# Row sums of softmax from added-up chunks: four chunks of E summed on Pool and split into two fp16 halves, in place of sixteen matmuls

## The chip, the cores and the metric

The kernel runs on one core of one Trainium2 chip. The metric is the device time of one execution in microseconds (us), median over several runs.

## The reference, cut to what matters

Attention with 8 batches and 12 heads, sequence 448, head size 64, then a gated feed-forward block on 3584 tokens with width 768 and inner width 1536. Inputs and output are fp32.

```python
def _attn_ref(q, k, v):
    scores = (1.0 / np.sqrt(q.shape[-1])) * np.matmul(q, k.transpose(0, 1, 3, 2))
    scores = scores - np.max(scores, axis=-1, keepdims=True)
    attn = np.exp(scores)
    attn = attn / (np.sum(attn, axis=-1, keepdims=True) + 1e-09)
    return np.matmul(attn, v)

def _moe_ref(x, w_gate, w_val, w_out):
    g = x @ w_gate
    silu = g * (1.0 / (1.0 + np.exp(-g)))
    return silu * (x @ w_val) @ w_out
```

## The kernel before

The 96 heads are taken in 48 pairs, one pair per turn of a loop of 50 turns. In a turn PE (the matmul engine, which takes its work in the program's order) makes the scores of the pair in two halves (QK), ScalarE (ACT) turns them into `E = exp(scores)` in fp16, and PE fills the time in between with steps of the feed-forward block of earlier batches (`ffn_run`). Two pairs make a "quad" of four heads. In even turns PE takes the row sums of a quad by multiplying `E` with ones, in odd turns it multiplies `E` with `v` (PV), and VectorE (DVE) scales the product with the reciprocal of the sums.

`E` has the key index on partitions, in four chunks of 112. So a row sum goes over partitions and over chunks: 4 chunks x 4 heads = 16 matmuls.

```python
    def sums(p0):
        acc = ps_f.tile([128, 512], FP32, tag="f")
        for c in range(NC):                      # 4 chunks
            for j in range(4):                   # 4 heads
                nc.tensor.matmul(acc[ts(j, 32), 0:S], lhsT=ones[:],
                    rhs=E[p0 + j // 2][:, c, j % 2, :],
                    start=(c == 0), stop=(c == NC - 1))
        R[p0] = attp.tile([128, S], FP32, tag="R", bufs=2, name="R")
        return acc

    def recips(p0, acc):
        ssb = attp.tile([128, S], FP32, tag="ssb", bufs=1)
        nc.vector.tensor_copy(ssb[:], acc[:, 0:S])
        rt = R[p0]
        return [lambda i=i: nc.vector.reciprocal(rt[:, ts(i, P)], ssb[:, ts(i, P)])
                for i in range(4)]
    # ... (cut)
        for pr in range(END):
            # ...
            if pr < NPAIR:
                qk_half(pr, 0, ...)
            if pr + 3 < NPAIR and pr + 3 >= NPE:
                prep(pr + 3)                     # Pool copies q and k of a later pair
            if not odd and 14 <= pr + LA < NPAIR:
                load_qk16(pr + LA)               # issued by Pool
            if pr + 2 < NPAIR:
                # ...
                if (pr + 2) % GP == GP - 1 and 4 <= (pr + 2) // GP + 1 < NGRP:
                    load_v((pr + 2) // GP + 1)   # issued by Pool, three buffers
            # ...
            elif not odd and pr >= 2:
                deferred.extend(recips(pr - 2, sums(pr - 2)))
            # ...
            work = odd and pr > FIRST + 1
            if work:
                pop_deferred(4)
                scaled(pr - 3, 0, pv(pr - 3, 0))
            # ...
            carry = ffn_run(state["left"] / slots + carry)
            # ...
                qk_half(pr, 1, ...)
            if work:
                scaled(pr - 3, 1, pv(pr - 3, 1))
            carry = ffn_run(state["left"] / max(1, slots - 1) + carry)
```

The softmax here doesn't subtract the row's maximum and nothing guards it: scores larger than these inputs give would overflow.

## Time and profile before

| before | value |
|---|---|
| time, median of 4 runs | 462.67 us (462.06 to 463.93) |
| span of the profiled run | 460.2 us |
| busy PE / VectorE / ACT / Pool | 452.3 / 236.8 / 243.0 / 104.2 us |
| PE idle (span less busy) | 7.9 us, nearly all in the first 30 us |

A line of the waits view names the engine and instruction that waited, what released it, and then total us, number of times and longest wait. This is all that PE waits for in the kernel before:

```profile
PE s L196 <- ACT E L203: 2.2, 5, 0.4
PE wp L103 <- DVE ones L355: 1.2, 1, 1.2
PE acc L234 <- ACT E L203: 0.4, 1, 0.4
PE s L196 <- DVE qkT L175: 0.2, 1, 0.2
```

The windows view gives the busy time of each engine in a stretch of time (instructions in brackets), then PEclk, the share of full speed that PE's clock was granted. For before, in two stretches of the later part:

```profile
85.00:113.00 28.00, 28.00 (x390) 11.82 (x382) 19.32 (x29) 16.64 (x22) 9.49 (x16) 1.00 1.08 140
113.00:167.00 54.00, 54.00 (x950) 28.05 (x952) 32.39 (x51) 30.94 (x44) 15.45 (x25) 1.00 0.70 93
```

PE (second number) is busy for every microsecond, at full clock; VectorE (fourth) is busy for 60 to 70%; Pool (sixth) for about 30%.

### The profile page before, as it was taken

Reading aid. Unit: us, or ns where it says so; the run is one execution under the profiler, and the core shown is the slowest. Engines: PE = TensorE matmul, PEld = TensorE weight load, DVE = VectorE, ACT = ScalarE, POOL = GpSimd, SP = SyncE. Lnnn points to the kernel's source line nnn. Section 1 sums busy time; section 2 is a strip of 40 time slices with the busy share of each in tenths; the row PEclk is TensorE's granted clock in tenths of the full one; section 3 lists DMA queues with packets and bytes.
Section 4 is the critical chain, followed back from the end, with each engine's and each line's share of the span. In section 5 each row is a group of like instructions: output and inputs, shape, how many; then the busy total and the mean of one; then the engine's idle time right before and its main releaser. Section 6 shows DMA issues by size and latency. Waiting matters only on the chain.

```text
span 460.2 us, 14133 instructions
## 1 busy us (share of the span) xinstructions
PE 452.3 (98%) x6367; PEld 227.8 (49%) x6367; DVE 236.8 (51%) x371; ACT 243.0 (53%) x353; POOL 104.2 (23%) x164
## 2 busy tenths in 40 slices
PE   8899999999999999999999999999999999999996
PEld 3344444444455555444455555544445556554454
DVE  2765663666764554564654554636555546334310
ACT  7986666656664555454646555455555562222222
POOL 8455606334150132303123040210200000000000
PEclk9999999999999999999999999999999999999999
DMA  9999999995793484662758393903603111100123
GB/s 133 195 200 201 192 180 183 223 154 80 90 113 57 78 126 49 114 102 31 118 58 119 67 131 74 142 6 76 98 10 56 37 37 36 36 11 25 36 68 103
DMA packets 82045, 44.23 MB, mean 96 GB/s; under 512 B 36673, under 2 KB 78529, under 8 KB 81985
## 3 DMA queue, kind: packets, MB, share of 16 engines
q0 software_dynamic: 42368, 23.37, 39.2%
q1 hardware_dynamic: 39520, 19.92, 23.8%
q8 instruction: 49, 0.80, 0.7%
q14 instruction: 12, 0.09, 0.1%
q10 hardware_dynamic: 96, 0.05, 0.0%
HBM read 47.19 MB, written 11.01 MB: 126 GB/s over the span
## 4 chain that ended last, share of the span: by engine, by line
PE 95%; ACT 3%; DMA 1%; DVE 0%; issue 0%; SPq 0%; ACTq 0%
PE gp L264 15%; PE op L261 14%; PE vp L264 13%; PE vp L261 11%; PE op L264 10%; PE s L196 10%; PE gp L261 9%; PE acc L212 9%; PE acc L234 4%; ACT E L203 2%; DMA rk<-in_k_dram 1%; PE tp L184 1%; PE wp L103 0%; PE tp L167 0%; DVE qkT L175 0%
## 5 line engine op out<-in xcount | busy, mean ns | idle before, releaser
L203 ACT ACTIVATE E<-s 112x896 f16<-112x896 f32 x192 | 164.6, 917 | 24.3 <-PE s L196 24.1
L280 ACT ACTIVATE sg<-gp 128x384 f32<-128x384 f32 (+1 forms) x96 | 52.3, 545 | 85.4 <-PE gp L264 54.7
L292 DVE SCALAR_TENSOR_TENSOR t<-sg,gp 128x384 f32<-128x384 f32 (+1 forms) x96 | 58.5, 610 | 64.3 <-ACT sg L280 64.2
L325 ACT ACTIVATE osb<-op 128x384 f32<-128x384 f32 (+1 forms) x57 | 27.7, 486 | 100.5 <-PE op L261 56.3
L264 PE MATMUL gp<-X,wg 128*32 128x512 f16 (+1 forms) x1416 | 78.1, 355 | 0.0
L249 DVE RECIPROCAL R<-ssb 128x112 f32<-128x112 f32 x92 | 73.1, 827 | 0.7
L295 DVE SCALAR_TENSOR_TENSOR hts<-t,vp 128x384 f16<-128x384 f32 (+1 forms) x96 | 59.6, 621 | 23.3 <-PE vp L264 7.9
L261 PE MATMUL op<-wo,hts 128*128 128x384 f16 (+1 forms) x408 | 68.6, 322 | 0.0
L264 PE MATMUL vp<-X,wv 128*32 128x512 f16 (+1 forms) x1224 | 66.9, 353 | 0.0
L226 DVE TENSOR_TENSOR X<-acc,R 128x448 f16<-128x448 f32 x48 | 29.7, 624 | 64.9 <-PE acc L212 63.1
L261 PE MATMUL vp<-X,wv 128*128 128x384 f16 (+1 forms) x270 | 58.4, 352 | 0.0
L196 PE MATMUL s<-qkT 64*128 64x448 f16 x384 | 54.8, 355 | 2.5 <-ACT E L203 2.2
L261 PEld LDWEIGHTS <-hts 128*128 128x128 f16 x408 | 38.9, 98 | 28.2 <-issue 3.0
L264 PEld LDWEIGHTS <-wg 128*32 128x32 f16 x1416 | 37.8, 97 | 29.6
L264 PE MATMUL op<-wo,hts 128*32 128x384 f16 x1104 | 48.9, 326 | 0.0
L261 PE MATMUL gp<-X,wg 128*128 128x384 f16 (+1 forms) x222 | 47.4, 350 | 0.0
L264 PEld LDWEIGHTS <-wv 128*32 128x32 f16 x1224 | 32.7, 97 | 25.5
L212 PE MATMUL acc<-E,vt 112*32 112x448 f16 x768 | 45.2, 355 | 0.0
L126 POOL DMA_DIRECT2D vt<-in_v_dram x16 | 12.3, 772 | 142.7 <-PE acc L212 141.7
L261 PEld LDWEIGHTS <-wv 128*128 128x128 f16 x270 | 25.3, 98 | 26.9 <-issue 4.8
L264 PEld LDWEIGHTS <-hts 128*32 128x32 f16 x1104 | 29.5, 97 | 16.3
L154 POOL COPY qk<-q 112x512 f16<-112x512 f16 x37 | 22.9, 620 | 63.9 <-DMA qkT<-qk 46.4
(38 smaller groups left out, 201.2 us busy)
## 6 DMA issues: line engine op xcount, KB each, us to landing
vt<-in_v_dram POOLq DMA_DIRECT2D x16, 336.0 KB, 5.2
q<-in_q_dram POOLq DMA_DIRECT2D x22, 224.0 KB, 5.9
k<-in_k_dram POOLq DMA_DIRECT2D x22, 224.0 KB, 6.7
out_dram<-osb SPq DMA_DIRECT2D x7, 336.0 KB, 3.1
wg<-in_moe_w_gate_dram POOLq DMA_DIRECT2D x8, 288.0 KB, 11.1
wv<-in_moe_w_val_dram POOLq DMA_DIRECT2D x8, 288.0 KB, 11.4
wo<-in_moe_w_out_dram POOLq DMA_DIRECT2D x2, 1152.0 KB, 21.6
out_dram<-osb SPq DMA_DIRECT2D x8, 288.0 KB, 2.9
```

The costliest lines, as they stand in the source:

```text
L154: nc.gpsimd.tensor_copy(dst, src)
L196: nc.tensor.matmul(s[:, hx, 0:S], lhsT=t[ts(hx, 64)].rearrange("p c q -> p (c q)")[:, c * P : c * P + 128], rhs=t[ts(hx, 64), NC:, :].rear ...
L203: nc.scalar.activation(E[pr][:, c], s[0:P, :, 0:S], AF.Exp, scale=sm_scale)
L212: nc.tensor.matmul(acc[ts(j, 32), 0:S], lhsT=v16[g][:, 2 * r + j % 2, c, :].rearrange("p (d t) -> p t d", t=2)[:, t], rhs=E[p0 + j // 2][: ...
L226: nc.vector.tensor_tensor(X[kk][:, hp + t, ts(bb, S)], acc[:, 0:S], R[p0][:], ALU.mult)
L249: lambda i=i: nc.vector.reciprocal(rt[:, ts(i, P)], ssb[:, ts(i, P)]) for i in range(4)
L261: nc.tensor.matmul(dst, lhsT=lhsT, rhs=rhs, start=start, stop=stop)
L264: nc.tensor.matmul(dst[ts(j, 32), :], lhsT=lhsT[:, ts(j, 32)], rhs=rhs, start=start, stop=stop)
L280: nc.scalar.activation(sg[:, 0:n], gp[:, 0:n], AF.Tanh, scale=0.5)
L292: nc.vector.scalar_tensor_tensor(t1[:, 0:n], sg[:, 0:n], 1.0, gp[:, 0:n], ALU.add, ALU.mult)
L295: nc.vector.scalar_tensor_tensor(hts[:, fb, 0:n], t1[:, 0:n], 0.5 * HS, vp[:, 0:n], ALU.mult, ALU.mult)
L325: nc.scalar.activation(osb[:, ds(m0, w)], op[:, 0:w], AF.Copy, scale=1.0 / HS)
```

## The change

The intent is to take row-sum work off PE, the bound. For pairs 12 to 47 the four chunks of a head are first added elementwise on Pool in fp32. The sum is then written as two fp16 halves, because the row-sum matmuls here read fp16: ACT rounds a quarter of it (`hi`), VectorE makes the remainder (`lo`), and PE multiplies both with 4.0. That takes 8 matmuls rather than 16. To give this chain time, sums and PV of the later quads come one turn later (odd and even change places). To give Pool time, the copies of q and k go to VectorE. Space in SBUF is found by smaller buffers (RB 5 to 4, no `t1`), and k of pair 0 is loaded on ACT's queue.

```diff
-RB = 5
+RB = 4
+PS = 12
@@ copies of q and k in prep
-                    nc.gpsimd.tensor_copy(dst, src)
+                    (nc.vector if pr >= PS + 3 else nc.gpsimd).tensor_copy(dst, src)
@@
+    def presum_a(pr):
+        ts_ = [attp.tile([P, S], FP32, tag="tsum", bufs=3, name="tsum") for _ in range(2)]
+        tsum[pr] = ts_
+        for hx in range(2):
+            nc.gpsimd.tensor_tensor(ts_[hx][:], E[pr][:, 0, hx], E[pr][:, 1, hx], ALU.add)
+
+    def presum_b(pr):
+        for hx in range(2):
+            t = tsum[pr][hx]
+            for c in (2, 3):
+                nc.gpsimd.tensor_tensor(t[:], t[:], E[pr][:, c, hx], ALU.add)
+
+    def presum_hi(pr):
+        hl[pr] = attp.tile([P, 2, 2, S], FP16, tag="hl", bufs=2, name="hl")
+        for hx in range(2):
+            nc.scalar.activation(hl[pr][:, 0, hx], tsum[pr][hx][:], AF.Copy, scale=0.25)
+
+    def presum_lo(pr, hx):
+        nc.vector.scalar_tensor_tensor(
+            hl[pr][:, 1, hx], tsum[pr][hx][:], 0.25, hl[pr][:, 0, hx], ALU.mult, ALU.subtract
+        )
@@ in sums(): n chunks rather than NC
+        pre = p0 >= PS
+        n = 2 if pre else NC
+                src = hl[p0 + j // 2] if pre else E[p0 + j // 2]
@@ the loop
+            elif odd and pr >= PS + 3 and pr - 3 < NPAIR:
+                pop_deferred(99)
+                deferred.extend(recips(pr - 3, sums(pr - 3)))
+            if PS < pr <= NPAIR:
+                presum_b(pr - 1)
-            work = odd and pr > FIRST + 1
+            quad = None
+            if odd and FIRST + 1 < pr < PS + 3:
+                quad = pr - 3
+            if not odd and pr >= PS + 4:
+                quad = pr - 4
+            work = quad is not None
@@ after the second half of PV
+            if PS <= pr < NPAIR:
+                presum_a(pr)
+            if PS < pr <= NPAIR:
+                presum_hi(pr - 1)
+                for hx in range(2):
+                    deferred.append(lambda p=pr - 1, hx=hx: presum_lo(p, hx))
@@ (cut: END = NPAIR + 3, add_at one turn later, t1 replaced by sg, ones with a 4.0, loads of pair 0 and of q16/k16 rearranged)
```

More of the change, by code (lines that the diff above doesn't have):

```diff
@@ L64, in load_table @@
         )
-    load_table("natural_log_exp_and_others")
     consts = ctx.enter_context(tc.tile_pool(name="consts", bufs=1))
@@ L77 @@
     ps_f = ctx.enter_context(tc.tile_pool(name="ps_f", bufs=3, space=PSUM))
-    ones = consts.tile([P, 32], FP16, name="ones")
-    warm = consts.tile([128, 512], FP16, name="warm")
+    ones = consts.tile([P, 2, 32], FP16, name="ones")
+    warm = ep.tile([128, 512], FP16, tag="E", name="warm")
     ident = consts.tile([P, P], FP16, name="ident")
@@ L93 @@
     raw = {}
+    pairbuf = []
+    tsum = {}
+    hl = {}
     v16 = {}
@@ L107, in load_qk32 @@
         rk = raws.tile([P, 2, NC, D], FP32, tag="rk", bufs=RB)
-        for dst, src in ((rq, q), (rk, k)):
-            nc.sync.dma_start(dst[:], src[0, 2 * pr : 2 * pr + 2].rearrange("h (p c) d -> p h (c d)", c=NC))
+        for dst, src, eng in ((rq, q, nc.sync), (rk, k, nc.scalar)):
+            eng.dma_start(dst[:], src[0, 2 * pr : 2 * pr + 2].rearrange("h (p c) d -> p h (c d)", c=NC))
         raw[pr] = (rq[:], rk[:])
     def load_qk16(pr, n=2):
-        q16 = raws.tile([P, 4, NC, D], FP16, tag="rq", bufs=RB, name="q16")
-        k16 = raws.tile([P, 4, NC, D], FP16, tag="rk", bufs=RB, name="k16")
-        for dst, src in ((q16, q), (k16, k)):
+        h0 = 2 if pr == 2 else 0
+        if h0 == 0:
+            pairbuf.clear()
+            for tag in ("rq", "rk"):
+                pairbuf.append(raws.tile([P, 4, NC, D], FP16, tag=tag, bufs=RB, name=tag))
+        for dst, src in zip(pairbuf, (q, k)):
             flat = src.rearrange("b h s d -> (b h) s d")[2 * pr : 2 * pr + 2 * n]
-            nc.gpsimd.dma_start(dst[:, 0 : 2 * n], flat.rearrange("h (p c) d -> p h (c d)", c=NC))
+            nc.gpsimd.dma_start(
+                dst[:, h0 : h0 + 2 * n], flat.rearrange("h (p c) d -> p h (c d)", c=NC)
+            )
         for i in range(n):
-            raw[pr + i] = (q16[:, 2 * i : 2 * i + 2], k16[:, 2 * i : 2 * i + 2])
+            raw[pr + i] = tuple(x[:, h0 + 2 * i : h0 + 2 * i + 2] for x in pairbuf)
     def load_v(g, lo=0, hi=2 * GP):
@@ L228, in scaled @@
         )
+    def presum_a(pr):
[15 more added lines that the diff above has]
+            hl[pr][:, 1, hx], tsum[pr][hx][:], 0.25, hl[pr][:, 0, hx], ALU.mult, ALU.subtract
+        )
     def sums(p0):
         acc = ps_f.tile([128, 512], FP32, tag="f")
-        for c in range(NC):
+        pre = p0 >= PS
+        n = 2 if pre else NC
+        for c in range(n):
             for j in range(4):
+                src = hl[p0 + j // 2] if pre else E[p0 + j // 2]
                 nc.tensor.matmul(
                     acc[ts(j, 32), 0:S],
-                    lhsT=ones[:],
-                    rhs=E[p0 + j // 2][:, c, j % 2, :],
+                    lhsT=ones[:, int(pre)],
+                    rhs=src[:, c, j % 2, :],
                     start=(c == 0),
-                    stop=(c == NC - 1),
+                    stop=(c == n - 1),
                 )
@@ L290, in ffn1_steps @@
                 )
-            t1 = fp.tile([128, 512], FP32, tag="t1")
             nc.vector.scalar_tensor_tensor(
-                t1[:, 0:n], sg[:, 0:n], 1.0, gp[:, 0:n], ALU.add, ALU.mult
+                sg[:, 0:n], sg[:, 0:n], 1.0, gp[:, 0:n], ALU.add, ALU.mult
             )
             nc.vector.scalar_tensor_tensor(
-                hts[:, fb, 0:n], t1[:, 0:n], 0.5 * HS, vp[:, 0:n], ALU.mult, ALU.mult
+                hts[:, fb, 0:n], sg[:, 0:n], 0.5 * HS, vp[:, 0:n], ALU.mult, ALU.mult
             )
@@ L353 @@
         load_qk32(0)
+        load_table("natural_log_exp_and_others")
         nc.vector.memset(warm[:], 0.0)
-        nc.vector.memset(ones[:], 1.0)
+        nc.vector.memset(ones[:, 0], 1.0)
+        nc.vector.memset(ones[:, 1], 4.0)
         load_qk16(1, 1)
@@ L428 @@
         carry = 0.0
-        DELAY = 2
-        END = NPAIR + 2
+        END = NPAIR + 3
         add_at = {FIRST: 0}
         for i in range(1, B - 1):
-            add_at[NHP * (i + 1) + DELAY] = i
+            add_at[NHP * (i + 1) + (2 if NHP * i + 4 < PS else 3)] = i
         for pr in range(END):
@@ L461 @@
                 ffn_run(2.5)
-            elif not odd and pr >= 2:
+            elif not odd and 2 <= pr < PS + 2:
                 deferred.extend(recips(pr - 2, sums(pr - 2)))
@@ L470 @@
                     scaled(pr - 3, t, halves[t])
-            work = odd and pr > FIRST + 1
+            if PS < pr <= NPAIR:
[6 more added lines that the diff above has]
+            work = quad is not None
             if work:
-                pop_deferred(4)
-                scaled(pr - 3, 0, pv(pr - 3, 0))
+                pop_deferred(99)
+                scaled(quad, 0, pv(quad, 0))
             if pr in add_at and pr != FIRST:
@@ L495 @@
             if work:
-                scaled(pr - 3, 1, pv(pr - 3, 1))
+                scaled(quad, 1, pv(quad, 1))
+            if PS <= pr < NPAIR:
[4 more added lines that the diff above has]
+                    deferred.append(lambda p=pr - 1, hx=hx: presum_lo(p, hx))
             tiled[0] = pr >= TILED and work
```

## The prediction

> **What bounds the kernel now.** I read first the table of busy time and the page's chain that ended last, then the waits of PE and of Pool, then the timelines of PE and Pool in the middle of the run.
>
> ```profile
> PE 452.3 (98%) x6367; PEld 227.8 (49%) x6367; DVE 236.8 (51%) x371; ACT 243.0 (53%) x353; POOL 104.2 (23%) x164
> PE 95%; ACT 3%; DMA 1%; DVE 0%; issue 0%; SPq 0%; ACTq 0%
> ```
>
> The chain is PE for 95% of the span. Since a busy PE need not be an efficient one, I checked with the waits of PE: they add up to 4.0 us (exponentials 2.6, a memset 1.2, a copy 0.2), and in the window from 30 us to the end there is none at all. After the first 28 us, in which the exponentials pace the chain, every microsecond taken from PE shortens the run and every microsecond for which PE is made to wait lengthens it: there is no slack to absorb either.
>
> The row sums in PE's timeline (start us, length us; four chunks times four heads are the 16 matmuls):
>
> ```profile
> 158.05 0.55 PE L196 MATMUL s<-qkT 64*128 64x448 f16 x4
> 158.53 0.94 PE L212 MATMUL acc<-E,vt 112*32 112x448 f16 x16
> 159.30 2.13 PE L264 MATMUL op<-wo,hts 128*32 128x384 f16 x48
> 161.25 1.15 PE L264 MATMUL vp<-X,wv 128*32 128x384 f16 x24
> 162.33 0.55 PE L196 MATMUL s<-qkT 64*128 64x448 f16 x4
> 162.81 0.94 PE L234 MATMUL acc<-E,ones 112*32 112x448 f16 x16
> ```
>
> Lengths overlap, so I take start to start: a set of sums (L234) 162.81 to 163.58, where the next group starts, 0.77 us; PV is also 0.77, a gate or value step of 384 columns 0.98 (1.30 of 512), an output step 1.95, a QK half 0.5. A pair (one turn of the loop) takes some 9 us.
>
> Pool in the same stretch (the bracket is the idle time before):
>
> ```profile
> 159.77 0.77 POOL L126 DMA_DIRECT2D vt<-in_v_dram  x1 [27.42 <-PE acc L212]
> 160.53 0.62 POOL L154 COPY qk<-q 112x512 f16<-112x512 f16 x1
> 161.08 0.62 POOL L154 COPY qk<-k 112x512 f16<-112x512 f16 x1
> ```
>
> This is the row that decides my prediction. Pool stood for 27 us at the issue of a V load until the last PV that reads the old V buffer was over (159.30 on PE; 0.47 us later the issue starts), and the copies behind it had to stand too. Pool's waits give 141.7 us in 9 such places. Today this costs nothing, since Pool is 23% busy and what stands behind is needed much later.
>
> **What the Trainium skill says.** (1) "GPSIMD Engine Reference", section 3.1: a two-input tensor_tensor costs about 2.6 cycles per element at 1.2 GHz (4497 ns for 2048 fp32), a one-input body 1.03. The trace agrees with the second: copies of 512 start 555 ns apart, 439 ns of which is 512 x 1.03 / 1.2, leaving 116 ns for the instruction. The first the trace before can't test, as it has no two-input Pool instruction. Estimate for 448 elements: 448 x 2.55 / 1.2 + 116 = 1070 ns. (2) "SBUF — State Buffer", section "Who interferes with whom": a VectorE instruction with two SBUF inputs, or in a 2-port mode, and a GpSimd instruction that reads SBUF block each other for a whole instruction. Before, no costly VectorE group has two SBUF inputs, so the trace doesn't show it. (3) "TensorE: Matmul & The Clock Gate", Part 1: after an idle window of about 3.4 us the clock falls to half. The trace has PEclk at 9 throughout and no PE wait over 1.2 us, so it is silent too.
>
> **The change part by part.** Eighteen quads (pairs 12 to 47) get their sums from 8 matmuls instead of 16: 384 become 240. Saved on PE: 18 x 0.77 / 2 = **6.9 us**, all on the path. At the start, k goes out on ACT's queue beside q: the cast of k waited until 4.30 us against 3.59 for q, and VectorE is busy with q until 3.98, so some **0.3 us**. Wider gaps elsewhere: none; the feed-forward work is only shifted by one pair.
>
> Added off PE: Pool 216 adds x 1.07 = 231 us, less 66 copies x 0.62 = 41 that go to VectorE, so Pool rises to about 294 us. Per 9 us pair that is 6 x 1.07 + about 1.0 of DMA issue = 7.4 us: full, but below the bound. ACT 72 copies x 0.58 (the nearest row is 128x448 at 577 ns) = 42 us, to 285. VectorE 72 subtractions x 0.6 = 43 plus 66 copies x about 0.3 = 20, to 300. By sums of busy time nothing passes PE, and one would expect about 455.
>
> The order of instructions says otherwise. A pair's last four adds (its two remaining chunks, two heads) stand on Pool **behind the V load** of their turn. In turns 18, 24, 30, 36 and 42 that load waits for the second PV half of the very same turn, because PV of the new quads now comes one turn later (in turn p+4 instead of p+3) while the V load and its three buffers stayed. And these four adds are needed by the row sums early in the next turn. So a chain appears, from the end of that PV: release 0.47 + V issue 0.77 + four adds 4.28 + ACT's rounding to fp16 0.6 + VectorE's remainder 0.6 with some 0.5 of blocking by Pool = 7.2 us, then the sums on PE. Meanwhile PE has in its fixed order, by the program:
>
> - turn 18: value and gate steps of 512 columns, QK: 1.30 + 1.30 + 0.5 = 3.1, wait 4.1
> - turns 30 and 42: value of 512, output, QK: 1.30 + 1.95 + 0.5 = 3.8, wait 3.4 each
> - turns 24 and 36: output, value (2.9), then a gate step whose PSUM buffer is freed by an ACT copy that stands behind the two rounding copies: 0.47 + 0.77 + 4.28 + 0.6 + 0.5 = 6.6, wait 3.7 each
>
> Sum: 4.1 + 2 x 3.4 + 2 x 3.7 = **18.3 us** of new PE idle time.
>
> A second, weaker loop: three sum buffers for two heads a pair make the second first-add of a pair wait for the previous pair's remainder, which on VectorE stands behind reciprocals; in even turns the issue of q and k (1.4 us) comes between. Turn by turn this mostly fits into the 9 us; in the shortest, turn 20 (6.6 us of PE work), I count a wait of up to 3.8 us. I put **2 us** in for all of this, a choice: the other turns could add to it, and VectorE may be earlier than I think.
>
> Sum: 462.5 - 6.9 - 0.3 + 18.3 + 2 = 475.6; I say **475 us**.
>
> **The rivals.**
> (a) *All hidden.* The adds are much faster than my estimate. At 0.5 us each the chain of the V load is 4.9 us, its waits shrink to about 1.8, 1.1, 1.1 and twice 1.4, in all 7 us, and the run takes some 462; at 0.3 us it is nearly hidden, 457 or so. For it: sums of busy time leave room everywhere, and the change looks as if its author thought of latency (sums and PV come later, casts leave Pool). Against it: the copy's 555 ns for one input, and the page's rate for two.
> (b) *The shared port.* Per pair VectorE has two subtractions with two SBUF inputs and two copies that may need the port while Pool is at it for 6.4 us; every one can lose up to 1.07 us, so VectorE 300 + 36 x 4 x 0.5 = 372 us. Then remainders and feed-forward products come late as well, PSUM buffers come free late, and the time is 480 to 490. For it: the page. Against: VectorE's total still lies under PE's.
> (c) *The clock falls* after those idle times of over 3.4 us: 5 times up to 1.7 us more, near 484. For it: their length; against: they are just at the page's window.
> (d) *Pool becomes the bound*: it needs the adds at 1.35 us or more (6 x 1.35 + 1.0 = 9.1 per pair). Then over 480.
>
> **Range and chances.** The step that carries all is the length of an add: a tenth of a microsecond of it is worth 4 x 5 x 0.1 = 2 us. With 0.3 to 0.5 us we are at 456 to 462, with 0.9 to 1.2 at 472 to 480, with (b) or (c) up to 490. Range 455 to 490. Faster by over 2% means below 453.3, more than the 7.2 us that there is to win: 0.05. Within 2% is rival (a), which an author who measured would have wanted to see: 0.35. Slower (above 471.8): 0.60.
>
> **What would show it.** Right: PE's waits list the sums' matmuls waiting for VectorE or ACT, about 3 to 4 us in each of five places some 54 us apart, with a V issue on Pool just before; the mean of a Pool tensor_tensor is about 1.07 us; the chain runs through Pool in those places; a set of sums takes about 0.39 us start to start. Wrong: adds of under 0.5 us, or PE without waits after 30 us; then the time is 455 to 460. If the waits of PE are spread over all turns instead of five, the second loop or the shared port was the larger term; a PEclk below 9 after the gaps would be rival (c).

## The result, and the profile after

| | before | after |
|---|---|---|
| median | 462.67 us | 516.94 us (514.85 to 519.04, 4 runs) |
| span of the profiled run | 460.2 us | 515.0 us |
| PE busy / idle | 452.3 / 7.9 us | 469.6 / 45.4 us |
| VectorE busy | 236.8 us | 334.3 us |
| ACT busy | 243.0 us | 275.1 us |
| Pool busy | 104.2 us | 302.0 us |
| mean granted clock | 1.00 | 0.966 |

The ratio is 1.1169, 95% interval 1.1118 to 1.122: slower by 11.7%. A ratio here is always the mean time of one kernel's runs over that of the other's runs of the same rounds, so it isn't quite the ratio of the medians quoted.

The prediction said slower, but 475 us and at most 490. Of the 54.8 us by which the span grew, 37.5 are PE's idle time (45.4 less 7.9) and 17.3 are more busy time. PE's busy time should have fallen by 6.9, so some 24 us of slower work are hidden in it. One part is the clock (below). The matmuls' ends are modelled, so another part may be a tail put on the last matmul ahead of each wait; that is not shown.

The chain that ended last, by engine, in the kernel after:

```profile
PE 65%; DVE 12%; POOL 10%; ACT 7%; issue 4%; DMA 1%; POOLq 0%; DVEq 0%; ACTq 0%
```

Before, PE had 95% of it. The three largest waits of PE after:

```profile
PE acc L267 <- ACT hl L253: 12.8, 8, 2.0
PE acc L267 <- DVE hl L256: 10.2, 10, 3.3
PE gp L297 <- ACT osb L357: 7.4, 2, 3.7
```

L267 is the matmul of the row sums, L253 the rounding, L256 the remainder. Their 23.0 us are waits for the new chain. The 7.4 us on `osb` are the two turns that the prediction gave 3.7 us each, at its very numbers. Added up by place from PE's timeline, the five turns with a V load wait 2.8, 3.7, 2.5, 3.7 and 2.5 = 15.2 us (predicted 18.3). But some 20 us lie in other turns, where I had counted 2.

First such a turn with a V load, turn 18. Pool (start us, length, then what; the bracket is the idle time before and what ended it):

```profile
126.72 0.77 POOL L134 DMA_DIRECT2D vt<-in_v_dram  x1 [1.03 <-PE acc L220]
127.50 4.51 POOL L248 TENSOR_TENSOR tsum<-tsum,E 112x448 f32<-112x448 f32 x4
```

And PE in the same stretch:

```profile
125.69 0.74 PE L220 MATMUL acc<-E,vt 112*32 112x448 f16 x12
126.25 1.47 PE L297 MATMUL vp<-X,wv 128*32 128x512 f16 x24
127.55 1.47 PE L297 MATMUL gp<-X,wg 128*32 128x512 f16 x24
128.95 0.55 PE L204 MATMUL s<-qkT 64*128 64x448 f16 x4
129.43 0.37 PE L267 MATMUL acc<-hl,ones 112*32 112x448 f16 x2
130.32 0.35 PE L267 MATMUL acc<-hl,ones 112*32 112x448 f16 x1 [0.52 <-ACT hl L253]
132.68 0.56 PE L267 MATMUL acc<-hl,ones 112*32 112x448 f16 x4 [2.01 <-ACT hl L253]
133.54 0.53 PE L267 MATMUL acc<-hl,ones 112*32 112x448 f16 x1 [0.30 <-DVE hl L256]
133.55 2.75 PE L297 MATMUL vp<-X,wv 128*32 128x512 f16 x23
```

PV ends, Pool issues the V load, makes four additions, and only then come rounding, remainder and sums. PE has value, gate and QK in between, as predicted, and waits. The last row shows a second loss: the value step (23 of its 24 matmuls lie in the stretch) takes 2.75 us where the same step took 1.47 seven rows above.

Now a turn without a V load, turn 17, on PE:

```profile
110.99 0.37 PE L267 MATMUL acc<-hl,ones 112*32 112x448 f16 x4 [2.01 <-ACT hl L253]
113.83 0.53 PE L267 MATMUL acc<-hl,ones 112*32 112x448 f16 x1 [2.47 <-DVE hl L256]
113.84 3.09 PE L297 MATMUL gp<-X,wg 128*32 128x512 f16 x24
116.37 2.76 PE L297 MATMUL vp<-X,wv 128*32 128x512 f16 x24
```

PE waits 2.0 us for a rounding and 2.5 us for a remainder, and the two feed-forward steps behind them start 2.5 us apart instead of 1.30. The windows view says why (first number after the comma PE's busy time, PEclk is third from the end); the stretches are cut where the granted clock changes:

```profile
108.40:111.81 3.41, 0.95 (x9) 0.29 (x8) 1.19 (x2) 1.63 (x4) 3.33 (x4) 1.00 0.18 24
111.81:118.63 6.82, 4.80 (x48) 2.61 (x48) 6.03 (x8) 1.82 (x3) 5.85 (x6) 0.50 0.37 22
118.63:122.00 3.37, 3.37 (x35) 1.12 (x30) 2.83 (x6) 2.53 (x4) 0.00 (x0) 1.00 0.14 29
```

The clock was at half from 111.81 to 118.63 us. It fell 0.4 us into the second wait, so the first wait and the little work around it were enough. The whole run has seven such falls, ahead of the drop at its end: in the five turns with a V load, in turn 17 and in turn 21. They begin at 111.81, 132.29, 152.77, 197.14, 258.58, 320.02 and 381.46 us, whole multiples of 3.41 us apart, and in the 3.41 us ahead of each PE was busy for 0.00 to 1.40 us. Two such slots in turn 15, with 1.67 and 2.00 us of work, were not followed by a fall. In all the clock was at half for 34.1 us, and PE was busy for 27.6 of them; so, as an estimate, the clock cost PE at most 27.6 / 2 = 14 us of its own time.

Over the longer stretches shown of before, after has:

```profile
85.00:113.00 28.00, 20.17 (x257) 8.10 (x250) 19.02 (x29) 17.18 (x25) 24.40 (x25) 0.98 0.73 98
113.00:167.00 54.00, 45.00 (x523) 20.27 (x526) 40.40 (x60) 26.46 (x42) 37.89 (x39) 0.82 0.41 53
```

Last, the groups of instructions (busy us in total, mean ns of one, then idle time before them and what ended it):

```profile
L256 DVE SCALAR_TENSOR_TENSOR hl<-tsum,hl 112x448 f16<-112x448 f32 x72 | 53.6, 764 | 34.7 <-ACT hl L253 34.5
L162 DVE COPY qk<-rq 112x512 f16<-112x512 f16 x33 | 31.7, 962 | 1.9 <-DMA rq<-in_q_dram 1.9
...
L162 DVE COPY qk<-rk 112x512 f16<-112x512 f16 x33 | 25.1, 761 | 0.9 <-DMA rk<-in_k_dram 0.9
```

```profile
L253 ACT ACTIVATE hl<-tsum 112x448 f16<-112x448 f32 x72 | 39.4, 583 | 37.7 <-POOL tsum L248 37.6
```

```profile
L248 POOL TENSOR_TENSOR tsum<-tsum,E 112x448 f32<-112x448 f32 x144 | 153.4, 1076 | 5.9
L242 POOL TENSOR_TENSOR tsum<-E 112x448 f32<-112x448 f16 x72 | 84.2, 1176 | 75.0 <-DVE hl L256 75.0
```

An addition onto a sum (L248) takes 1076 ns (1070 predicted), a first addition (L242) 1176; the median of all is 1041. A copy of q takes 962 ns and one of k 761 on VectorE, where I had put 0.3 us. And Pool waits 75 us for remainders, which free the sum buffers: the second loop of the prediction is there. Read as a circle: first additions wait for remainders (75.0 us), roundings for additions (37.6 us), remainders for roundings (34.5 us).

### The profile page after: what moved, and what is told of

Same layout as the page of the kernel before. It is cut to its first block, busy times and chain, and to the rows that moved or that the text cites. A ratio compares the mean times of both kernels' runs of the same rounds, so it can differ in the third digit from the quotient of the medians.

```text
span 515.0 us, 14492 instructions
## 1 busy us (share of the span) xinstructions
PE 469.6 (91%) x6331; PEld 235.5 (46%) x6331; DVE 334.3 (65%) x510; ACT 275.1 (53%) x425; POOL 302.0 (59%) x314
## 4 chain that ended last, share of the span: by engine, by line
PE 65%; DVE 12%; POOL 10%; ACT 7%; issue 4%; DMA 1%; POOLq 0%; DVEq 0%; ACTq 0%
PE op L294 11%; PE gp L297 11%; PE vp L294 8%; POOL tsum L248 8%; PE vp L297 8%; PE gp L294 6%; PE s L204 6%; PE acc L220 6%; PE op L297 5%; ACT E L211 4%; DVE hl L256 3%; DVE qk L162 3%; PE acc L267 2%; ACT hl L253 2%; DVE sg L324 2%
## 5 line engine op out<-in xcount | busy, mean ns | idle before, releaser
L248 POOL TENSOR_TENSOR tsum<-tsum,E 112x448 f32<-112x448 f32 x144 | 153.4, 1076 | 5.9
L242 POOL TENSOR_TENSOR tsum<-E 112x448 f32<-112x448 f16 x72 | 84.2, 1176 | 75.0 <-DVE hl L256 75.0
L297 PE MATMUL gp<-X,wg 128*32 128x512 f16 (+1 forms) x1440 | 89.7, 380 | 11.8 <-ACT osb L357 7.4
L324 DVE SCALAR_TENSOR_TENSOR sg<-sg,gp 128x384 f32<-128x384 f32 (+1 forms) x96 | 58.0, 604 | 49.3 <-ACT sg L313 48.9
L297 PE MATMUL vp<-X,wv 128*32 128x512 f16 (+1 forms) x1296 | 77.1, 368 | 0.3 <-DVE ssb L279 0.3
L256 DVE SCALAR_TENSOR_TENSOR hl<-tsum,hl 112x448 f16<-112x448 f32 x72 | 53.6, 764 | 34.7 <-ACT hl L253 34.5
L327 DVE SCALAR_TENSOR_TENSOR hts<-sg,vp 128x384 f16<-128x384 f32 (+1 forms) x96 | 59.6, 621 | 15.9 <-PE vp L294 3.9
L357 ACT ACTIVATE osb<-op 128x384 f32<-128x384 f32 (+1 forms) x57 | 27.6, 483 | 78.2 <-PE op L294 45.6
L253 ACT ACTIVATE hl<-tsum 112x448 f16<-112x448 f32 x72 | 39.4, 583 | 37.7 <-POOL tsum L248 37.6
L294 PE MATMUL vp<-X,wv 128*128 128x512 f16 (+1 forms) x252 | 54.7, 354 | 0.0
L297 PEld LDWEIGHTS <-wv 128*32 128x32 f16 x1296 | 39.6, 101 | 30.2 <-issue 6.7
```

What stands on the lines that cost most here:

```text
L242: nc.gpsimd.tensor_tensor(ts_[hx][:], E[pr][:, 0, hx], E[pr][:, 1, hx], ALU.add)
L248: nc.gpsimd.tensor_tensor(t[:], t[:], E[pr][:, c, hx], ALU.add)
L256: nc.vector.scalar_tensor_tensor(hl[pr][:, 1, hx], tsum[pr][hx][:], 0.25, hl[pr][:, 0, hx], ALU.mult, ALU.subtract)
L294: nc.tensor.matmul(dst, lhsT=lhsT, rhs=rhs, start=start, stop=stop)
L297: nc.tensor.matmul(dst[ts(j, 32), :], lhsT=lhsT[:, ts(j, 32)], rhs=rhs, start=start, stop=stop)
L324: nc.vector.scalar_tensor_tensor(sg[:, 0:n], sg[:, 0:n], 1.0, gp[:, 0:n], ALU.add, ALU.mult)
```

## The experiments

The theories:

- **V load**: the V load ahead of the additions makes a chain, as predicted.
- **Buffers**: three sum buffers for two heads a pair tie Pool's first additions to the remainders of the pair before, and turns grow into each other.
- **Port**: Pool's additions and VectorE's copies and remainders block each other, VectorE's in-order queue runs late, and PE waits for it in all turns.
- **Clock**: waits make PE's clock fall, so each costs more than its length.

### The rest of the change alone

```diff
-PS = 12
+PS = 48
```

No pair takes the new way; the rearranged loads, buffers and the longer loop stay.

> The sums of all pairs taken by PE from the four chunks again, all other parts of the change kept (four raw buffers, in-place feed-forward product, k loaded on ACT's queue, table load later). Theory of the chain (PE waits for sums that Pool makes late): all 54 us come from the added-up sums, so this is back at 462 to 464. Rival (the other parts cost something of their own): over 467.

Correct, 462.44 us, ratio 0.9992 (0.9965 to 1.002). The rest of the change costs and gains nothing. The 0.3 us that the prediction wanted from the earlier load of k can't be seen: in the profiles the first row of exponentials started at 6.0 and 6.8 us in the two kernels with the old way of loading, and at 6.6 to 7.3 us in the others.

### The V load at the end of its turn

```diff
-                if (pr + 2) % GP == GP - 1 and 4 <= (pr + 2) // GP + 1 < NGRP:
+                if pr < PS and (pr + 2) % GP == GP - 1 and 4 <= (pr + 2) // GP + 1 < NGRP:
                     load_v((pr + 2) // GP + 1)
@@ ahead of the last ffn_run of the turn
+            if PS <= pr < NPAIR - 2 and pr % GP == 0 and (pr + 2) // GP + 1 < NGRP:
+                load_v((pr + 2) // GP + 1)
```

> The V load of a later turn issued at the end of its turn, behind the last four adds, not before them. Chain theory: the five places where PE waits after a V load (2.8, 3.7, 2.5, 3.7, 2.5 us, 15.2 in all) go, with the clock lost behind them (about 6 us): 493 to 500. The waits of the turns 14, 16 and 20 stay. Rival (the port shared by Pool and VectorE makes everything late): still 508 or more.

Correct, 497.79 us, ratio 1.0755 (1.0722 to 1.0787). Against the changed kernel that is 0.0414 of 463 us, or 19 us. The V load was worth what the prediction gave it (18.3), its waits of 15.2 us and some clock. But 35 us remain.

### Four sum buffers

```diff
-... tag="tsum", bufs=3 ...
+... tag="tsum", bufs=4 ...
-        ssb = attp.tile([128, S], FP32, tag="ssb", bufs=1)
-        nc.vector.tensor_copy(ssb[:], acc[:, 0:S])
         rt = R[p0]
+        nc.vector.tensor_copy(rt[:], acc[:, 0:S])
@@ the reciprocals read rt in place of ssb (to find the space)
```

> Four sum buffers in place of three (room made by taking the reciprocals in place), so that the second first-add of a pair no longer waits for the previous pair's remainder. Chain theory: Pool's 75 us of waiting for VectorE go, PE's waits in the turns 15, 17 and 21 (11.6 us and 2 at a gate step) and most of the lost clock there (up to 9.7 us) go, the V waits stay: 485 to 496. Rival (shared port): VectorE's copies and remainders are as late as before, 505 or more.

Correct, 514.90 us, ratio 1.1122 (1.108 to 1.1163). The expectation of 485 to 496 failed; the gain of 2 us isn't even certain, since the intervals overlap. So the 75 us that Pool waited for remainders did not by themselves cost the time: with Pool let go, VectorE's busy time rose from 334 to 351 us, and PE waited for other things.

### Both together

> Both at once. Chain theory: PE's waits after 30 us fall from some 38 us to under 6, the clock stays near 1.00, and the saving of 6.9 us on PE comes through: 455 to 466. Rival (shared port): PE still waits over 15 us for remainders, 480 or more.

Correct, 492.82 us, ratio 1.0642 (1.0616 to 1.0667). If the two loops were the cause, the time had to come near 460. With the V load out of the way the buffer is worth 5 us (1.0755 less 1.0642), no more. VectorE's busy time is now 359.9 us, and PE waits for the whole of VectorE's work:

```profile
PE gp L296 <- DVE sg L323: 8.5, 5, 2.1
PE acc L220 <- DVE X L234: 6.3, 5, 1.7
PE acc L267 <- DVE hl L256: 6.2, 7, 1.4
```

`sg` is a feed-forward product, `X` the scaling of PV: both were there before the change and were never late. The buffer theory is out as the main cause. The port theory had asked for 480 or more, which came, and for over 15 us of waits for remainders, which did not: there were 6.2, out of 22.3 for VectorE as a whole.

### Additions that nobody reads, and the same without them

Two kernels. Their outputs are wrong, which doesn't matter for the times. In the first, Pool makes all its additions, but rounding and remainder read a constant tile, so that no work waits for an addition:

```diff
+    fix = consts.tile([P, S], FP32, name="fix")      # set to 1.0 at the start
-            nc.scalar.activation(hl[pr][:, 0, hx], tsum[pr][hx][:], AF.Copy, scale=0.25)
+            nc.scalar.activation(hl[pr][:, 0, hx], fix[:], AF.Copy, scale=0.25)
-            hl[pr][:, 1, hx], tsum[pr][hx][:], 0.25, ...
+            hl[pr][:, 1, hx], fix[:], 0.25, ...
@@ the reciprocals in rt, as above
```

In the second, Pool's additions are taken out of this kernel:

```diff
-            if PS < pr <= NPAIR:
-                presum_b(pr - 1)
-            if PS <= pr < NPAIR:
-                presum_a(pr)
```

> Wrong result on purpose: ACT's rounding and VectorE's remainder read a constant tile, so nothing but loads waits for Pool's adds, which all still run; every instruction of the change is there. Theory of the shared port: copies of 0.25 us and remainders of 0.6 us on VectorE are still stretched to about 1.1 and 0.9 us, VectorE's busy time stays near 340 to 360 us, PE still waits for it: 470 to 485. Theory of latency alone (only waiting for the adds costs): 454 to 460.

> The same without Pool's 216 adds. Both theories: copies at about 0.25 us, remainders at 0.6 us, PE without waits after 30 us, 454 to 458. If it is over 462, the added ACT and VectorE instructions cost time by themselves, without any port.

With additions: 494.6 us, ratio 1.0669 (1.0639 to 1.07). Without: 462.29 us, ratio 0.9972 (0.9957 to 0.9987). The only difference is work on Pool whose result no other engine reads, and it costs 0.0697 of 463 us, or 32 us, more than the port theory had expected (470 to 485) and nowhere near its rival (454 to 460). VectorE with the additions:

```profile
L257 DVE SCALAR_TENSOR_TENSOR hl<-fix,hl 112x448 f16<-112x448 f32 x72 | 82.3, 1172 | 5.7 <-ACT hl L254 5.7
...
L324 DVE SCALAR_TENSOR_TENSOR sg<-sg,gp 128x384 f32<-128x384 f32 (+1 forms) x96 | 57.5, 599 | 41.7 <-ACT sg L313 41.6
...
L163 DVE COPY qk<-rq 112x512 f16<-112x512 f16 x33 | 28.9, 876 | 3.7 <-DMA rq<-in_q_dram 3.7
```

and without:

```profile
L324 DVE SCALAR_TENSOR_TENSOR sg<-sg,gp 128x384 f32<-128x384 f32 (+1 forms) x96 | 58.3, 607 | 53.0 <-ACT sg L313 52.9
L257 DVE SCALAR_TENSOR_TENSOR hl<-fix,hl 112x448 f16<-112x448 f32 x72 | 41.8, 612 | 7.8 <-ACT hl L254 7.8
...
L163 DVE COPY qk<-rq 112x512 f16<-112x512 f16 x33 | 9.4, 286 | 1.8 <-DMA rq<-in_q_dram 1.8
```

The remainder (two inputs from SBUF) takes 1172 ns beside the additions and 612 without, the copy 876 and 286. The product L324 with one input from SBUF and one from PSUM takes 599 and 607: it isn't touched. By busy time that is 70 us of VectorE in all (357.4 against 287.1). Total busy time still lies far below PE's, but not everywhere. The windows view of the kernel with additions:

```profile
85.00:113.00 28.00, 24.24 (x308) 10.33 (x312) 26.81 (x37) 18.93 (x29) 27.42 (x27) 1.00 0.69 114
113.00:167.00 54.00, 45.00 (x696) 21.53 (x689) 50.59 (x66) 29.98 (x47) 50.51 (x50) 0.97 0.48 73
```

VectorE is busy for 26.8 of 28 and 50.6 of 54 us there: it is the bound in these stretches, together with Pool, and PE loses 3.8 and 9.0 us. (Pool's queue also issues loads, and the additions delay these. The traces bound that rival: after the first 5 us no instruction of PE, ACT or VectorE waited for Pool, and only two of them for a load, both on VectorE at 72 to 74 us, for 4.3 us with the additions and 2.6 without. After the start PE's waits, 26.1 us, name VectorE but for 0.2 us. So the 32 us are put down to the blocking.)

Without additions the expectation was 454 to 458, since sums take 8 matmuls. Only 1 us of 6.9 arrived; a later run takes this up.

### The copies on ScalarE

On top of both buffers and the late V load:

```diff
-                    (nc.vector if pr >= PS + 3 else nc.gpsimd).tensor_copy(dst, src)
+                    if pr >= PS + 3:
+                        nc.scalar.activation(dst, src, AF.Copy)
+                    else:
+                        nc.gpsimd.tensor_copy(dst, src)
```

> On top of d_vlate_tsum4 (493 us) the 66 copies of q and k go from VectorE to ACT. Shared port: VectorE loses about 60 us of busy time, PE's waits for VectorE fall from 21 us to under 10: 472 to 482. If the copies do not matter: 489 or more.

Correct, 482.66 us, ratio 1.0406 (1.0388 to 1.0423): 11 us better than with the copies on VectorE (1.0642), just outside the 472 to 482 that the port theory asked for and away from its rival. The two parts behind it came short: VectorE's busy time fell by 46 us (359.9 to 314.1) rather than 60, and PE's waits for it from 22.3 to 14.4 us rather than to under 10. The remainders still took 1197 ns each, and PE waited 8.7 us for them and 3.5 us for `sg`.

### Throw-away matmuls in the waits

In the changed kernel, ahead of the sums of the first four new quads, 11, 22, 14 and 26 groups of four matmuls, 0.187 us a group, that the sums then overwrite:

```diff
+        for _ in range({12: 11, 14: 22, 16: 14, 18: 26}.get(p0, 0)):
+            for j in range(4):
+                nc.tensor.matmul(acc[ts(j, 32), 0:S], lhsT=ones[:, 0],
+                    rhs=E[p0 + j // 2][:, 0, j % 2, :], start=True, stop=True)
```

> The changed kernel with throw-away matmuls (2.0, 4.1, 2.6 and 4.9 us of them) ahead of the first four early sums, where PE otherwise waits 2.3, 4.5, 2.8 and 5.3 us. If the clock falls because PE waits, the clock stays near 1.00 up to 167 us, and the run is 7 to 11 us shorter than the changed kernel though PE has 13.6 us more to do: 505 to 510. If the clock falls for another reason, or PE's waits do not matter for it: 515 or more.

Correct, 512.53 us, ratio 1.105 (1.1026 to 1.1074): 5.5 us faster than the changed kernel with 13.6 us more work on PE. The windows view shows the clock in the stretch where it had been 0.82:

```profile
113.00:167.00 54.00, 50.20 (x798) 23.93 (x798) 43.12 (x64) 29.34 (x46) 42.72 (x43) 1.00 0.49 67
```

So the clock fell because of the waits (the three falls up to 167 us are gone, the four later ones, in turns that were not filled, are still there), and its fall in this stretch cost about 5.5 us by this run. The gain was smaller than expected (505 to 510 us), so the clock's whole share stays open beside the 14 us estimated above.

### Without rounding and remainder

The late V load, the copies on ScalarE, and Pool's last addition writes fp16 itself: no `hi`, no `lo`, and a quad's sums take 4 matmuls. The sums are now of fp16 precision.

```diff
+        hl[pr] = attp.tile([P, 1, 2, S], FP16, tag="hl", bufs=3, name="hl")
-            for c in (2, 3):
-                nc.gpsimd.tensor_tensor(t[:], t[:], E[pr][:, c, hx], ALU.add)
+            nc.gpsimd.tensor_tensor(t[:], t[:], E[pr][:, 2, hx], ALU.add)
+            nc.gpsimd.tensor_tensor(hl[pr][:, 0, hx], t[:], E[pr][:, 3, hx], ALU.add)
-                presum_hi(pr - 1)
-                for hx in range(2):
-                    deferred.append(lambda p=pr - 1, hx=hx: presum_lo(p, hx))
-        n = 2 if pre else NC
+        n = 1 if pre else NC
```

> The V load at the end of its turn, the casts of q and k on ScalarE, and Pool's last addition writes fp16 itself: no rounding on ScalarE, no remainder on VectorE, four matmuls for the row sums of a quad in place of eight. Theory of the shared port (VectorE is late because its copies and remainders lock with Pool's additions): VectorE has no such instruction left in the later pairs, so its busy time falls to some 240 us, PE has under 3 us of waits after 30 us, and PE saves 18 x 0.58 = 10 us against before: 452 to 458 us; if the saving fails to arrive as in the run without additions, 460 to 463. Rival: Pool is too slow by itself (a pair's six additions and the DMA issues take 7.4 us of a turn, and the order of the queues makes PE wait for them): waits for Pool in PE's list and over 466 us. Precision is worse than that of the change (fp16 sums), still expected to pass.

Correct, 459.58 us, ratio 0.993 (0.9907 to 0.9953). VectorE has nothing left that meets Pool: its busy time is 234.8 us, as before the change, while Pool still makes all its additions (busy 286.5 us). All that PE waits for in the new chain is this:

```profile
PE acc L271 <- POOL hl L252: 1.9, 3, 1.1
```

Against the kernel with late V load, four buffers and copies on ScalarE it is, though it has three buffers, 22 us faster (1.0406 less 0.993). Four matmuls fewer in each of 18 quads explain about 3 of them. So a busy Pool by itself costs PE next to nothing. Two things changed at once, though: VectorE's blocked instructions went, and the way from an addition to the sums got two engines shorter; this run does not tell how the 22 us divide. This kernel beats both, by 0.7% (clear of noise, but under the 2% at which a verdict is called) and by 11%, at a lower precision of the sums. The saving was to be 10 us and is 3; 459.58 lies between the two ranges expected.

### The same with the copies on VectorE

> As the run before this one, but the casts of q and k stay on VectorE as in the change. It measures the copies alone: with the shared port each of the 66 takes 0.8 to 1.1 us rather than 0.29, VectorE's busy time is 40 to 55 us above that of the run with the casts on ScalarE. If lateness of VectorE is what costs, 3 to 10 us longer than that run (VectorE has no remainder to do and so more room than in the run where the casts were worth 10 us); if only the additions' length mattered, the same within 1 us.

Correct, 460.78 us, ratio 0.9956 (0.9935 to 0.9976). The copies took 644 and 768 ns, VectorE's busy time was 275.4 us, 40.6 more; the time was 1.2 us more, with overlapping intervals. I had expected 3 to 10. The same copies cost 11 us in the kernel with remainders, where VectorE's busy time was 359.9. I read this as: blocking costs time where VectorE has little room left, so it isn't the microseconds lost that count, but whether the engine is near full when they are lost. It is not the only reading, since here no remainder stands behind the copies on the way to the sums either.

### Half the row sums, alone

The kernel before: the sums of pairs 12 to 47 are taken from two of the four chunks. Its output is wrong, which doesn't matter for the time.

```diff
-        for c in range(NC):
+        n = 2 if p0 >= 12 else NC
+        for c in range(n):
-                    stop=(c == NC - 1),
+                    stop=(c == n - 1),
```

> The kernel before with the row sums of pairs 12 to 47 taken from two of the four chunks only: wrong on purpose, 8 matmuls for 16 and nothing else. It measures PE's saving by itself. The prediction's 18 x 0.77 / 2 = 6.9 us all on the path: 455.6 to 456.6 us. Rival, suggested by the run without additions (462.3): half of it or less arrives, because something else paces the end or the groups of matmuls overlap: 459 to 463 us.

456.49 us, ratio 0.9863 (0.9838 to 0.9889): 6.3 us of the predicted 6.9. The saving on PE is real. The kernel without additions has the same number of row-sum matmuls and is 5.0 us slower (0.9972 less 0.9863). In the profiles half of that is PE idle (10.7 against 8.2 us) and half PE busy (449.5 against 447.1): after 28 us the sums' groups take 12.1 us against 10.0 from start to start, waits included, the QK groups 41.7 against 40.6. The waits view names 1.3 us of waits for remainders. A set of eight sums takes 0.53 us, where the prediction had 0.39. So the new way costs most of its gain even with no addition in it; by what, beyond these 1.3 us, I leave open.

## Why the prediction was wrong, point by point

**That it would be slower, through the V load: right.** The row that decided the prediction held: the V load waits for PV, four additions follow (4.5 us in turn 18, 4.28 worked out), and PE waits in five turns for 15.2 us where 18.3 were worked out. Moving the load gave 19 us back.

**The saving: right in size.** 6.9 us predicted; 6.3 measured alone. In the change itself it can't be seen, and in the new way without additions only about 1 us of it arrived (462.29 us).

**The length of an addition: right.** 1076 ns for 1070. The two are not quite of a kind: 1070 was worked out from start to start, and so counted it is 1.00 us for additions that follow at once on another, in the median, and 1.13 for the four of turn 18. That the trace before "agrees" with the page's 1.03 for one input was no test, since the 116 ns are just what that rate left over. Rival (a), fast additions, and rival (d), Pool as the bound, fell with it; the kernel with fp16 additions shows Pool 286.5 us busy and PE waiting 1.9 us for it.

**The step that failed** is the line "I put **2 us** in for all of this, a choice", with the argument put against rival (b): "VectorE's total still lies under PE's." The waits outside the five turns were some 20 us, and the blocking alone costs 32 us when nothing depends on the additions. The estimate of VectorE's busy time with blocking, 372 us in rival (b), was close (359.9 us in the kernel with both loops out of the way). What I sized wrongly is what a total of 360 us out of 490 does. In the kernel with unread additions VectorE is busy for 94 to 96% of the time between 85 and 167 us; it works in the program's order, and so feed-forward products, scalings and remainders all come late. In the change itself VectorE is busy for only 19.0 of 28 and 40.4 of 54 us there, because it in turn waits for roundings, and these for additions, and the lateness goes round: late remainder, late first additions (75.0 us of waits), late rounding, late remainder, and the sums and PE with them. With a fourth buffer and the late V load the circle closes through PE instead: Pool's additions wait 49.4 us for exponentials and none for remainders. Neither half does it alone: all additions without remainders cost next to nothing (459.58 us), and remainders without additions neither (462.29 us). "480 to 490" for rival (b) thus was too little; its own experiment gives 494.6, and with the V load on top the time is 517.

**The copies** were part of it: I put "about 0.3" us each and then allowed 0.5 us of loss. They took 0.76 to 0.96 us, so the loss was sized rightly and its effect was not. Moving them to ACT gave 11 us back.

**The second loop** exists (Pool waits 75 us for remainders) but its removal gave 2 us alone, within the intervals, and 5 us with the late V load. It moved the wait: Pool let go blocks VectorE more.

**The clock**, rival (c), was left out of the sum because the waits worked out were just at the page's window. The clock fell in all five of these places, and in two more, though only two of the waits were longer than 3.4 us: what went ahead of each fall was a slot of 3.41 us with at most 1.40 us of work. Filling four waits gave 5.5 us.

Added up: the V load 19 us, the blocking 32 us, to be compared with 54 us; PE's saving and what the new way costs without additions nearly cancel (462.29 us), and the clock's share is inside the first two. The two were measured in different kernels, so that they fit this well may be in part luck.

## What to carry to other kernels

Before moving work to Pool, list what VectorE does in the same stretch with two inputs from SBUF, or as an fp16 copy: each can be held up by a whole instruction of Pool's (1.04 us here), and the sum must fit into the stretch's time, not into the span. Judge an in-order engine by its fullest stretch; the same blocked copies cost 11 us beside a nearly full VectorE and about 1 us beside one with room. If a helper engine's result must pass through two more engines before it is used, look for a form in which the helper writes the final type itself: the kernel with that form was 22 us faster here, more than what the change was meant to gain.

## What the Trainium skill lacked or had wrong

- "SBUF — State Buffer", section "Who interferes with whom": what it says of VectorE's two-input instructions, its copies and its one-input instructions beside Pool was borne out (the last unchanged, 599 against 607 ns). It gives no way to turn it into a kernel's time. Here a two-input instruction of 612 ns took 1172 on average beside Pool additions of 1.04 us, and an fp16 copy of 286 ns took 644 to 962; and what this cost the kernel ranged from about 1 us to 32 us, least where VectorE had room.
- "TensorE: Matmul & The Clock Gate", Part 1: as a rule of thumb, one idle window of about 3.4 us is too lenient, since the window need not be empty. The changed kernel's falls lie whole multiples of 3.41 us apart, and in the 3.41 us ahead of each PE was busy for 0.00 to 1.40 us; in turn 17 the clock fell with waits of 2.0 and 0.4 us in that time. The page says that many short idles can make the clock swing, too, but not how much work in a window is enough to prevent it. Here 1.67 us was; over all runs here (30 falls) the slots ahead of a fall hold up to about 1.6 us of work, and those without a fall go down to about 1.4.
- "GPSIMD Engine Reference", section 3.1: right. Its rate plus the 0.116 us worked out per instruction gave 1.07 us; the additions took 1.04 us in the median (1.00 from start to start), for fp32 with fp16 and for two fp16 inputs alike, where the page measures fp32 only.
- No page that I found spells out that a DMA issued by Pool which waits for a buffer holds up all the compute behind it in Pool's queue. It cost 19 us here.
